# Second-layer and first-layer products in three float32r passes in place of a Strassen scheme in fp32

## The chip, the cores and the metric

The kernel runs on one core of a Trainium2 chip. The metric is the device time of one execution in microseconds; the kernel before takes 351.21 us (median of three runs, 351.08 to 351.37). A core has TensorE (PE; PEld is its weight load), VectorE (DVE), ScalarE (ACT), GpSimd (POOL) and SyncE (SP, which here only issues DMAs). SBUF is the working memory, 128 partitions wide; PSUM, in eight banks of 128 x 512 fp32, takes the results of TensorE.

## The reference

A Mamba-2 scan over 4 batches, 8 heads and 768 steps (head width 32, state width 16) makes a matrix of 3072 tokens by 256, and that goes through a feed-forward pair with SiLU between.

```python
for c in range(nc):
    cum = np.cumsum(log_a[:, :, sl], axis=-1)
    L = np.exp(cum[..., :, None] - cum[..., None, :]) * causal
    y_intra = einsum('bhij,bhjd->bhid', (Cc @ Bc^T) * L, xc)
    y_inter = einsum('bhin,bhnd->bhid', Cc, state) * exp(cum)[..., None]
    y[:, :, sl] = y_intra + y_inter
    state = decay_full * state + sum_j(Bc * xc * decay_from_j)
x = y.transpose(0, 2, 1, 3).reshape(3072, 256)
h = x @ w_in                       # 256 -> 2048
out = (h / (1 + np.exp(-h))) @ w_out   # 2048 -> 256
```

The two weights are given as 64-bit floats. The kernel loads their 32-bit words and rebuilds fp32 values on the chip.

## The kernel before

The tokens are cut into twelve **units** of 256 tokens (three a batch), and these into six **pairs**. Each unit passes three stages: the scan, which leaves `XM` (the 256 features by 256 tokens of the unit); the first layer with SiLU, which leaves `gT` (2048 by 256); and the second layer, whose result is transposed and stored.

The **scan** of a unit is a chain over all engines. `f_E0` clamps the decays `a` and `f_E1` makes the decay products E by scan instructions (L304); `f_P0`, `f_P1` make prefix products (L285, L291); `f_T` transposes B and C (L347) or, for units 0 to 2, `f_TP` does it on TensorE (L356); `f_B` and `f_C` scale them on GpSimd (L341, L373); `f_D0` and `f_G0` are the small products on TensorE (L391, L406); `f_S` carries the state (L432); `f_M` multiplies the mask in (L417); `f_Y` has the last products (L460, L469), and `f_X` copies the result out of PSUM (L482). One PSUM tile of four banks, `gy`, serves all of this.

The **weights** come in sixteen pieces, eight of `w_in` and eight of `w_out`. `load_w` issues one DMA of 512 KB for a piece (L156). `w_size` takes the exponent half and the mantissa half on ScalarE (L164, L168). `w_bits` has three VectorE steps (L176, L178, L180) and one GpSimd add (L184). At most seven raw pieces are in memory (`RAW = 7`): the load of piece n + 7 stands behind `w_bits(n)`, and waits for it.

The **first layer** of units 0 to 3 is plain (`f_s1`, L505): per group of 256 of the 2048 features four fp32 products, then one SiLU from PSUM (L507). From pair 2 on `f_x1` takes the two units of a pair as a 2 x 2 block matrix and uses Strassen's seven products in place of eight (L703), with sums of weights (`f_SW`) and sums of inputs (`f_XT`, L686) made beforehand; the results are put together by adds from PSUM (L706), ScalarE copies (L717) and SiLU (L709).

The **second layer** is Strassen's scheme for all six pairs (`s2_pair`, L611 and L648): seven chains of eight products. It needs sums of `gT`: `f_T1` makes TN on VectorE (L544), and `f_TS` adds blocks in place, mostly by a DMA of GpSimd's queue that accumulates (L553). The seven results are copied out (L588), added on GpSimd (L558), transposed by VectorE (L564) and stored from SP (L566). The last pair's chains are arranged to end in short pieces (L626 to L639).

The order is written out by hand (`manual_schedule`): each engine takes its instructions in the order in which the Python code reaches them. Up to L867 the scan of units 0 and 1, the first weight pieces and the first groups are interleaved. The list `steps` (L869) then gives for each first-layer group of units 0 and 1 what follows it: `s6` is `w_size(6)`, `b5` is `w_bits(5)`, letters are stages of unit 2's scan. After that, two loops of eight and one over the pairs 2 to 5 mix the first layer of a pair, the second layer of the pair before (`f_s2(n)` gives n of its products) and the scan of the next one. `load_unit(u)` puts a unit's eleven to seventeen loads on SP's queue. All of SP's DMAs run in order, and a DMA waits until the one eight places earlier has landed.

Of the kernel before, what the change touches and what calls it, by code (L numbers as in the profile page):

```python
# [8 lines left out]
FP32 = mybir.dt.float32  # L9
U32 = mybir.dt.uint32  # L10
# [7 lines left out]
MOST = 2.0 ** 16 * (1.875 - 2.0 ** -22)  # L18


@with_exitstack
def kernel(
# [10 lines left out]

# [4 lines left out]
    Q = 64  # L49
    UT = 256  # L50
    UPB = S // UT
    NU = batch * UPB
    d_model, d_ff = moe_w_in.shape
# [5 lines left out]
    loads = ctx.enter_context(tc.tile_pool(name="loads", bufs=3))  # L59
    loads2 = ctx.enter_context(tc.tile_pool(name="loads2", bufs=2))  # L60
    rawp = ctx.enter_context(tc.tile_pool(name="rawp", bufs=7))
    wtp = ctx.enter_context(tc.tile_pool(name="wtp", bufs=3))
    sc = ctx.enter_context(tc.tile_pool(name="sc", bufs=1))
    sc2 = ctx.enter_context(tc.tile_pool(name="sc2", bufs=2))
    xmp = ctx.enter_context(tc.tile_pool(name="xmp", bufs=4))
    gpool = ctx.enter_context(tc.tile_pool(name="gpool", bufs=4))
    tpool = ctx.enter_context(tc.tile_pool(name="tpool", bufs=1))
    ppool = ctx.enter_context(tc.tile_pool(name="ppool", bufs=5))
    opool = ctx.enter_context(tc.tile_pool(name="opool", bufs=2))
    ps_s = ctx.enter_context(tc.tile_pool(name="ps_s", bufs=1, space=bass.MemoryType.PSUM))  # L70
    ps_h = ctx.enter_context(tc.tile_pool(name="ps_h", bufs=3, space=bass.MemoryType.PSUM))
    ps_o = ctx.enter_context(tc.tile_pool(name="ps_o", bufs=1, space=bass.MemoryType.PSUM))

    ctx.enter_context(tc.manual_schedule())


    pa, ab, bn, tbc, xt = ({} for _ in range(5))
# [4 lines left out]
    def load_pa(u, q):  # L82

        b, t0 = at(u)
        pa[u] = loads.tile([128, UT], FP32, name="pa")
# [3 lines left out]
    def load_ab(u, q):  # L89

        b, t0 = at(u)
        ab[u] = loads2.tile([128, 2, H, Q], FP32, name="ab")
# [6 lines left out]
    def load_n(u, i, q):  # L99

        b, t0 = at(u)
        if i == 0:
            t = bn[u] = loads.tile([128, 2, H, N], FP32, name="bn")
        else:
            t = tbc[u] = loads.tile([128, 2, 2, 8, N], FP32, name="tbc")[:, 0]
# [3 lines left out]
    def load_t(u, i, q):  # L109

        b, t0 = at(u)
        if u not in tbc:
            tbc[u] = loads.tile([128, 2, 2, 8, N], FP32, name="tbc")
# [4 lines left out]
    def load_x(u, q):  # L118
        b, t0 = at(u)
        xt[u] = loads.tile([128, 2, H, D], FP32, name="xt")  # L120
# [3 lines left out]
    def load_unit(u):  # L124
        load_pa(u, nc.sync)
        if 0 < u < UPB:
            load_n(u, 1, nc.sync)
        else:
            load_t(u, 0, nc.sync)
            load_t(u, 1, nc.sync)  # L130
# [39 lines left out]
    def w_bits(n, parts=1):  # L170
# [14 lines left out]
        if n + RAW < len(W):  # L185
            load_w(n + RAW, nc.sync)

# [820 lines left out]
```

## Time and profile before

| what | value |
|---|---|
| median of three runs | 351.21 us (351.08 to 351.37) |
| span of the profiled execution | 348.7 us |
| TensorE busy | 342.7 us, 98% |
| VectorE, ScalarE, GpSimd busy | 204.6, 162.8, 113.0 us |
| DMA traffic | 42.66 MB, 16.25 MB of it on GpSimd's queue |

The span runs from the first to the last instruction; the time measured for a run is 2.5 us above it, and the profiled execution's own time beside that is not recorded. In the profile a line such as `69.80 1.73 PE hp L505 x8` gives start, length, engine, tile written, line and count. An fp32 product appears as two records, so x8 is four products. A group's mean duration is that of single instructions, which overlap on TensorE: there the distance from start to start is the price. What stands in brackets is the idle time before, and what ended it.

### The profile page before, as it was taken

How to read it: one execution, taken by the hardware profiler on the slowest of the kernel's cores; microseconds unless marked ns; L12 is line 12 of the kernel's file. 1: busy time of each engine (PE TensorE's matmuls, PEld its weight loads, DVE VectorE, ACT ScalarE, POOL GpSimd, SP SyncE). 2: the span in 40 equal slices, each digit the busy share in tenths (PEclk: the TensorE clock that was granted, in tenths of full speed). 3: DMA queues.
4: the chain of work that ended last, by engine and by line, in shares of the span. 5: the costliest groups of instructions: out<-in, count | busy, mean ns of one | idle time of the engine just before them, and what ended most of it. 6: DMA issues, size and time to landing. Idle time of an engine off the chain costs nothing.

```text
span 348.7 us, 8382 instructions
## 1 busy us (share of the span) xinstructions
PE 342.7 (98%) x3324; PEld 288.5 (83%) x3324; DVE 204.6 (59%) x406; ACT 162.8 (47%) x399; POOL 113.0 (32%) x140
## 2 busy tenths in 40 slices
PE   8999999999999999999999999999999999999996
PEld 3678888888888888888888888888888888888886
DVE  7998799976795664544663563564652241233912
ACT  3578395323323545455645454644545454454010
POOL 4355245444285032244042244042235112041200
DMA  6877997799857598948178965056604237512202
GB/s 130 203 237 174 241 313 126 132 199 218 144 102 126 124 186 149 169 102 138 21 159 163 187 112 90 16 98 125 115 2 75 39 60 144 107 24 53 41 7 46
DMA packets 117056, 42.66 MB, mean 122 GB/s; under 512 B 102424, under 2 KB 108824, under 8 KB 117016
## 3 DMA queue, kind: packets, MB, share of 16 engines
q1 hardware_dynamic: 110472, 25.73, 35.8%
q0 software_dynamic: 4464, 16.25, 25.0%
q8 instruction: 26, 0.43, 0.6%
q10 hardware_dynamic: 2080, 0.13, 0.4%
q14 instruction: 14, 0.11, 0.1%
HBM read 22.70 MB, written 3.15 MB: 74 GB/s over the span
## 4 chain that ended last, share of the span: by engine, by line
PE 96%; DVE 1%; issue 1%; POOL 1%; ACT 0%; DVEq 0%; POOLq 0%
PE o_ps L648 36%; PE hp L703 28%; PE hp L505 16%; PE hp L648 3%; PE gy L469 2%; PE gy L406 2%; PE o_ps L611 2%; PE gy L460 2%; PE gy L391 1%; PE hp L626 1%; PE hp L312 1%; PE o_ps L226 1%; POOL w_in_sb L184 1%; DVE E L417 0%; PE o_ps L228 0%
## 5 line engine op out<-in xcount | busy, mean ns | idle before, releaser
L706 DVE TENSOR_TENSOR gT<-hp,p 128x256 f32<-128x256 f32 x64 | 26.9, 420 | 73.6 <-ACT p L717 37.6
L648 PE MATMUL o_ps<-gT,w_out_sb 128*128 128x256 f32 x240 | 60.4, 379 | 0.0
L709 ACT ACTIVATE gT<-gT 128x256 f32<-128x256 f32 x96 | 39.7, 414 | 43.9 <-DVE gT L706 43.9
L505 PE MATMUL hp<-XM,w_in_sb 128*128 128x256 f32 x256 | 59.3, 381 | 0.9 <-ACT XM L482 0.5
L505 PEld LDWEIGHTS hp<-XM,w_in_sb 128*128 128x128 f32 x256 | 48.0, 190 | 8.7 <-POOL w_in_sb L184 1.4
L703 PE MATMUL hp<-raw 128*128 128x256 f32 x192 | 52.7, 380 | 0.0
L558 POOL TENSOR_TENSOR ps<-ps 128x256 f32<-128x256 f32 x35 | 29.6, 845 | 71.1 <-ACT ps L588 69.8
L648 PEld LDWEIGHTS o_ps<-gT,w_out_sb 128*128 128x128 f32 x240 | 45.4, 190 | 6.3
L553 POOL DMA_DIRECT2D gT<-gT x31 | 27.9, 929 | 65.7 <-DVE TN L544 21.5
L703 PEld LDWEIGHTS hp<-raw 128*128 128x128 f32 x192 | 36.2, 190 | 5.4 <-POOL ps L558 0.6
L717 ACT ACTIVATE p<-hp 128x256 f32<-128x256 f32 x64 | 24.6, 384 | 27.4 <-PE hp L703 25.9
L706 DVE TENSOR_TENSOR gT<-hp,u 128x256 f32<-128x256 f32 x32 | 13.6, 424 | 38.6 <-PE hp L703 38.6
L703 PE MATMUL hp<-XM,w_in_sb 128*128 128x256 f32 x128 | 34.1, 389 | 0.0
L507 ACT ACTIVATE gT<-hp 128x512 f32<-128x512 f32 x32 | 18.9, 595 | 26.4 <-PE hp L505 26.3
L703 PEld LDWEIGHTS hp<-XM,w_in_sb 128*128 128x128 f32 x128 | 23.3, 190 | 4.3 <-issue 1.0
L304 DVE TENSOR_TENSOR_SCAN E<-ab,diag 128x256 f32<-128x256 f32 (+1 forms) x32 | 25.1, 826 | 0.8 <-DVE ab L323 0.5
L341 POOL TENSOR_TENSOR BT<-bn,E 128x256 f32<-128x256 f32 x12 | 9.4, 780 | 47.5 <-DVE E L304 39.4
L648 PE MATMUL o_ps<-gT,wu 128*128 128x256 f32 x88 | 22.4, 380 | 0.0
L648 PE MATMUL o_ps<-gT,wv 128*128 128x256 f32 x88 | 22.2, 380 | 0.0
L648 PE MATMUL o_ps<-gT,raw 128*128 128x256 f32 x80 | 20.5, 380 | 0.0
L588 ACT ACTIVATE ps<-o_ps 128x256 f32<-128x256 f32 x35 | 13.3, 383 | 14.8 <-PE o_ps L648 13.0
L703 PE MATMUL hp<-raw,w_in_sb 128*128 128x256 f32 x64 | 19.1, 380 | 0.0
(126 smaller groups left out, 522.3 us busy)
## 6 DMA issues: line engine op xcount, KB each, us to landing
gT<-gT POOLq DMA_DIRECT2D x31, 512.0 KB, 6.3
ab<-in_a_dram SPq DMA_DIRECT2D x40, 128.0 KB, 3.1
raw<-in_moe_w_in_dram SPq DMA_DIRECT2D x8, 512.0 KB, 5.1
raw<-in_moe_w_out_dram SPq DMA_DIRECT2D x8, 512.0 KB, 6.5
xt<-in_x_dram SPq DMA_DIRECT2D x24, 128.0 KB, 5.1
out_dram<-ot SPq DMA_DIRECT2D x92, 32.0 KB, 2.6
bn<-in_B_dram SPq DMA_DIRECT2D x22, 64.0 KB, 5.3
tbc<-in_C_dram SPq DMA_DIRECT2D x40, 32.0 KB, 3.4
```

The source lines that it names most:

```text
L304: nc.vector.tensor_tensor_scan(out=E[u].rearrange("p k h t -> p (k h t)")[:, Q * g0:Q * (g0 + n)], data0=t.rearrange("p g t -> p (g t)"), ...
L341: engine.tensor_tensor(out=BT[u], in0=bn[u], in1=E[u][:, :, :, Q - 1:Q].to_broadcast([128, 2, H, N]), op=ALU.mult)
L505: nc.tensor.matmul(out=hp[:, i], lhsT=w_in_sb[:, kc, f * 128:(f + 1) * 128], rhs=xm[:, kc], start=(kc == 0), stop=(kc == KC - 1))
L507: nc.scalar.activation(GTS[g][:, :, j], hp, AF.Silu)
L553: nc.gpsimd.dma_start(out=o[:, js], in_=a[:, js], accum_op=ALU.add)
L558: engine.tensor_tensor(out=o, in0=p, in1=q, op=op)
L588: nc.scalar.activation(p[m].rearrange("p (k c t) -> p c k t", c=2, k=2), o.rearrange("p (c k t) -> p c k t", c=2, k=2), AF.Copy)
L648: nc.tensor.matmul(out=o, lhsT=w(j), rhs=g()[:, j], start=(j == 0), stop=(j == last))
L703: nc.tensor.matmul(out=o, lhsT=w, rhs=x_, start=start, stop=True, skip_group_check=True)
L706: nc.vector.tensor_tensor(out=o, in0=p, in1=q, op=ALU.add)
L709: nc.scalar.activation(o, i, AF.Silu)
L717: nc.scalar.activation(o, i, AF.Copy)
```

## The change

The units, the scan's arithmetic and the rebuilding of the weights stay. Strassen's scheme goes in both layers. Pair 0 uses plain fp32 products in both layers (`f_s1` L463, `f_s2` L476). For the pairs 1 to 5 every operand is cut into parts of 12 bits that a float32r product can take exactly. For a weight w: `wh` is w times a scale, rounded to float32r (ScalarE, L178), `wl` is the rest (VectorE, L182), and `wd` is `wh - wl` (GpSimd, L186). For an activation: `XH`, `XL`, `XD` in the first layer (L444, L448, L452) and `GH`, `GL`, `GD` in the second (L538 or L540, L544, L546). The sum is then made of three products, `wd*XD`, `wh*XH` and `wl*XL`, of 512 columns each: the two units of a pair side by side. As the parts have different scales, the PSUM bank is rescaled in place by ScalarE between them: in the first layer once for each 128 features (L524), in the second layer after each half of the 16 chunks and between its parts (L557).

PSUM now has two banks for the first layer (three before) and two for the second (one before). SBUF tiles of 128 x 512 come from one pool of 77. The clamp of the decays moves from VectorE to GpSimd (L301), and E is made in place of its input. Raw weight pieces come as two DMAs of 256 KB, at most six pieces are asked for in advance (`RAW = 6`), and piece n + 6 is issued where `w_bits(n)` stands. Stores take 128 x 512 tiles (L494, L496).

The order is new too. `steps` has the digits of `w_in` (`D0` to `D7`) and unit 3's scan in the stage of pair 0; half of pair 0's second layer follows, the other half lies beside the first four of pair 1's sixteen groups, as do `D8` to `D15` beside its first eight. From there each group has the first product `ff1_r` of the next group, the other two of its own (`ff1_p`), the digits of the group before (`g_h`, `g_ld`), one of eight steps of a later unit's scan, and five to seven products of the second layer (`quota`), which runs five groups behind.

```diff
-    rawp = ctx.enter_context(tc.tile_pool(name="rawp", bufs=7))
-    ps_h = ctx.enter_context(tc.tile_pool(name="ps_h", bufs=3, space=bass.MemoryType.PSUM))
-    ps_o = ctx.enter_context(tc.tile_pool(name="ps_o", bufs=1, space=bass.MemoryType.PSUM))
+    ps_h = ctx.enter_context(tc.tile_pool(name="ps_h", bufs=2, space=bass.MemoryType.PSUM))
+    ps_o = ctx.enter_context(tc.tile_pool(name="ps_o", bufs=2, space=bass.MemoryType.PSUM))
...
-    RAW = 7
+    RAW = 6
...
+        raw[n] = [t2("raw").bitcast(U32).rearrange("p (f two) -> p f two", two=2) for k in range(2)]
+        for k in range(2):
+            q.dma_start(out=raw[n][k].rearrange("p f two -> p (f two)"), in_=src[:, k].bitcast(U32))
...
+    def w_h(n):
+        nc.scalar.activation(wh[n], w32[n], AF.Copy, scale=HS / BB)
+    def w_l(n):
+        nc.vector.scalar_tensor_tensor(out=wl[n], in0=f32(wh[n]), scalar=-BB, in1=w32[n], op0=ALU.mult, op1=ALU.add)
+    def w_d(n):
+        nc.gpsimd.tensor_tensor(out=wd[n], in0=f32(wh[n]), in1=f32(wl[n]), op=ALU.subtract)
...
-        nc.vector.tensor_scalar(out=t, in0=t, scalar1=1.0, scalar2=1e-6, op0=ALU.min, op1=ALU.max)
-        nc.vector.memset(t[:, :, 0:1], 0.0)
+        nc.gpsimd.tensor_scalar(out=t, in0=t, scalar1=1.0, scalar2=1e-6, op0=ALU.min, op1=ALU.max)
+        nc.gpsimd.memset(t[:, :, 0:1], 0.0)
...
+    def f_XH(u):
+        nc.scalar.activation(XH[p][:, :, v], XM[u], AF.Copy, scale=HS)
+    def f_XL(u):
+        nc.gpsimd.tensor_tensor(out=XL[p][:, :, v], in0=XM[u], in1=f32(XH[p][:, :, v]), op=ALU.subtract)
+    def f_XD(u):
+        nc.vector.scalar_tensor_tensor(out=XD[p][:, :, v], in0=f32(XH[p][:, :, v]), scalar=-CC, in1=XM.pop(u),
+                                       op0=ALU.mult, op1=ALU.add)
...
+    def ff1_r(p, j):
+        o = HP[p, j] = ps_h.tile([128, 512], FP32, name="hp")
+        for kc in range(KC):
+            nc.tensor.matmul(out=o, lhsT=w1(wd, j, kc), rhs=xx(XD, p, kc), start=(kc == 0), stop=(kc == KC - 1),
+                             skip_group_check=True)
+        nc.scalar.activation(o, o, AF.Copy, scale=1.0 / CC)
+    def ff1_p(p, j):
+        o = HP.pop((p, j))
+        for n, (w, v) in enumerate(((wh, XH), (wl, XL))):
+            for kc in range(KC):
+                nc.tensor.matmul(out=o, lhsT=w1(w, j, kc), rhs=xx(v, p, kc), start=False, stop=(n + kc == 2),
+                                 skip_group_check=True)
+        A[p, j] = t2("ga")
+        nc.scalar.activation(A[p, j], o, AF.Silu, scale=BB * CC)
+    def g_h(p, j):
+        GH[p, j] = t2("gh", F32R)
+        if j % 2:
+            nc.vector.tensor_scalar(out=GH[p, j], in0=A[p, j], scalar1=HS, scalar2=None, op0=ALU.mult)
+        else:
+            nc.scalar.activation(GH[p, j], A[p, j], AF.Copy, scale=HS)
+    def g_ld(p, j):
+        nc.gpsimd.tensor_tensor(out=GL[p, j], in0=A[p, j], in1=f32(GH[p, j]), op=ALU.subtract)
+        nc.vector.scalar_tensor_tensor(out=GD[p, j], in0=f32(GH[p, j]), scalar=-CC, in1=A.pop((p, j)),
+                                       op0=ALU.mult, op1=ALU.add)
+    def ff2(p):
...
+            for c, m in order:
+                mm(wh, GH[p, c], c, m, start=(c == 0))
+                yield
+                mm(wl, GL[p, c], c, m)
+                if c == cs[-1]:
+                    scale(m, CC)
+                yield
+            for m in range(2):
+                for c in cs:
+                    mm(wd, GD[p, c], c, m)
+                    if c == cs[-1]:
+                        if half:
+                            f_out(p, m, o[m], BB)
+                        else:
+                            scale(m, 1.0 / CC)
+                    yield
...
-    steps = ((1, 0, ""), (0, 3, "b5 s6"), (1, 1, "b6 s7"), (1, 2, "b7 s8"), (1, 3, "b8"), (0, 4, ""),
-             (1, 4, "T"), (0, 5, "E D s9"), (1, 5, "C b9 s10"), (0, 6, ""), (1, 6, "G b10 s11"),
-             (0, 7, "b11 s12"), (1, 7, "Y b12 s13"))
+    steps = ((1, 0, ""), (0, 3, "b5 s6"), (1, 1, "b6 s7"), (1, 2, "L3 b7 s8"), (1, 3, "b8 s9 P2"), (0, 4, "T2 D0"),
+             (1, 4, "E2 D1"), (0, 5, "b9 s10"), (1, 5, "D2 G2"), (0, 6, "b10 s11 D3"), (1, 6, "P3 Y2"),
+             (0, 7, "T3 D4"), (1, 7, "E3 D5"))
...
+    for c, what in enumerate(("b11 s12", "D6 G3", "b12 s13", "D7", "Y3", "b13 s14", "b14 s15", "b15")):
+        f_s2(c)
+        todo(what)
```

## The prediction

> **What bounds the kernel now.** First the page: engine shares, the 40 slices, the chain's shares. Then groups split by shape, for the duration of every operation named below. Then the chain in order of time, for the length of one pair of units. Then the time order of VectorE, GpSimd, ScalarE and the DMA queue from 20 to 70 us, because the slices show VectorE near full there.
>
> ```profile
> PE 342.7 (98%) x3324; PEld 288.5 (83%) x3324; DVE 204.6 (59%) x406; ACT 162.8 (47%) x399; POOL 113.0 (32%) x140
> PE   8999999999999999999999999999999999999996
> DVE  7998799976795664544663563564652241233912
> PE 96%; DVE 1%; issue 1%; POOL 1%; ACT 0%; DVEq 0%; POOLq 0%
> ```
>
> TensorE is the bound from end to end; VectorE is nearly full only in the first fifth.
>
> ```profile
> 69.80 1.73 PE hp L505 x8
> 131.56 1.06 PE hp L703 x4
> 185.57 1.06 PE hp L703 x4
> 239.50 1.06 PE hp L703 x4
> ```
>
> Eight records in 1.73 us are 0.2157 us each. An fp32 product with 256 columns has two records: 0.431 us. Equal points of three pairs lie 54.01 and 53.93 us apart. A Strassen pair's 112 products are 48.3 us and its two units' scans 2 x 2.42 (1.00 for L391 and L406, 1.42 for L460 and L469, by their starts); some 0.8 is left.
>
> ```profile
> 47.68 0.42 DVE L176 TENSOR_SCALAR wu<-wu 128x512 f32<-128x512 f32 x1
> 48.13 0.43 DVE L178 TENSOR_SCALAR wu<-wu 128x512 uint32<-128x512 uint32 x1
> 49.08 0.42 DVE L176 TENSOR_SCALAR wu<-wu 128x512 f32<-128x512 f32 x1
> 49.53 1.39 DVE L178 TENSOR_SCALAR wu<-wu 128x512 uint32<-128x512 uint32 x1
> ```
> ```profile
> 49.24 1.40 POOL L184 TENSOR_TENSOR w_out_sb<-wu,wv 128x512 uint32<-128x512 uint32 x1 [2.32 <-DVE wv L180]
> ```
>
> The same VectorE instruction takes 0.43 us alone and 1.39 when a GpSimd add (1.40) begins before it: it waits for the rest of that add, some 0.95.
>
> ```profile
> 24.15 0.42 SPq L156 DMA_DIRECT2D raw<-in_moe_w_out_dram  x1
> 24.62 1.35 SPq L86 DMA_DIRECT2D pa<-in_a_dram  x1
> 28.80 4.91 SPq L107 DMA_DIRECT2D bn<-in_B_dram  x2
> 37.90 4.99 SPq L156 DMA_DIRECT2D raw<-in_moe_w_out_dram  x7
> ```
> ```profile
> 43.37 0.67 ACT L164 ACTIVATE wu<-raw 128x512 f32<-128x512 f32 x1 [3.35 <-DMA raw<-in_moe_w_out_dram]
> ```
>
> Weight piece 8 goes out at 24.15, then unit 2's loads take 13 us of SP's queue, and piece 9 goes out at 37.90 and lands 5.5 us later, with ScalarE waiting 3.35.
>
> **Products.** Before there are 688 fp32 products (four units' first layer of 64 per pair, 56 per Strassen pair of each layer): 296.7 us. After, pair 0 has 128 plain ones (55.2 us) and each of the five other pairs 16 x 6 + 16 x 2 x 3 = 192 float32r products of 512 columns. No row shows float32r. Its floor is the one-pass bf16 128x512 (three in 0.81 us, L226, 0.22 each); its ceiling the fp32 record, two array steps a column, 0.43 for 512. I take one pass, 0.2157: with operands of 12 bits one pass is all that the sum needs, and each fp32 record already carries two of four. Then 207.1 us, together 262.3: **-34.5** (pair 0 +3.5, pair 1 -10.4, the others -6.9 each). The ceiling is a rival below. Weight loads (190 ns, L648) stay under a 0.216 us product as now; were they not hidden, 960 x at most 0.19.
>
> The Trainium skill, "FP8 and Floating Point Precision", on precision, says that true FP32 takes four passes and that a reduced form reads 4-byte values cut to 22 bits; four passes agree with 0.431 us. By its reduced form a 512-column product would cost a quarter of the pass time, 0.216 us.
>
> **The first pair.** It ends where the first float32r product (L522) starts. For TensorE alone: from 15.04 us, 16 first-layer groups of 1.73 (27.7), eight second-layer chunks of 1.73 (13.8), scans of units 1 to 3 (7.3), transposes and the present gaps some 1.8: 65.6 us. VectorE will be later, for two reasons.
>
> (a) Piece 8. Raw pieces in flight fall from 7 to 6, so in program order piece 8 now stands behind unit 2's eleven loads. They took 24.62 to 37.90 in the queue; without piece 8's 0.5 MB, up to 2.4 us less at the 218 GB/s of 10 to 20 us. So it is issued at 35.1 to 37.5 and lands 5.5 later, 41.8. ScalarE's piece-8 step stands ahead of the SiLU of group (1,3), at about 33.8, so ScalarE waits some 8 us, and with two PSUM banks for the first layer in place of three TensorE stops one group later. VectorE, done with piece 7 at 34 to 35, waits too. Piece 8's first VectorE step then starts at 42.3.
>
> (b) VectorE's list from there to the masked product of unit 3 (L379): four pieces at 1.5 unblocked (6.0), two prefix scans (2.0), seven low-part steps L182 priced by L180 (0.60 each by starts: 4.2), eight scans of E (4.9), C 0.35, two transposes 1.1, states 1.8, four masked products 2.4, one XD 0.6: 23.4. GpSimd now also makes wd, XL and the clamp of E (L301), so eleven of these steps find it at work: nine at 0.95 and two at 0.5, 9.6. Waiting for ScalarE's first wh, 1.8. Sum 34.8, so 77.1. Behind it stand unit 3's Y (1.4) and three chunks (5.2): L522 starts at 83.7, **+18** over 65.6. The floor is +5 (piece 8 on time and steps with two SBUF inputs not blocked), the ceiling +22 (all of it, the clamp at the 2.35 of the 1024-wide GpSimd add; its floor is twice the 0.67 affine_select, 1.3).
>
> **Pair 1.** Groups 4 to 7 (no fp32 chunks beside them: 1.3, 2.6, 3.6, 2.8 us of TensorE) still carry wl and wd. GpSimd: four GL and four wd at 1.28, BT and CW 1.3, clamp 1.3, and 3 us of waiting: 15.8 against 10.3. Up to one group (2.6) is covered by the distance from GL to its use: **+3**, between 0 and +5.
>
> **Pairs 2 to 5.** Per group 12 products, 2.59 us. Per pair, TensorE 46.3. ScalarE: 16 x (rescale 0.60, SiLU 0.60, half the high parts 0.30) by L507, six PSUM passes 3.6, scan copies 6.3: 34. No row writes PSUM from ScalarE; below 0.60 no row goes, and 0.1 more each would be 1.6 a pair, hidden: ten products (2.16 us) lie between L522 and L530 of the same group. VectorE: GD 16 x 0.68, GH 8 x 0.42, scans and the rest 17.5: 32. GpSimd: 16 GL and two XL at 1.28, four small 2.6, two clamps 2.6: 28. Each alone is hidden. Blocked time: 38 VectorE steps, GpSimd at work half the time, half an add left on average, 11 us; VectorE then 43 of 46.3. That is nearly full, and Y waits for VectorE's masked product, so I take 0.5 us a pair: **+2**, between 0 and 29 (if all 24 us of GpSimd's reads block VectorE: 53.5 a pair, +7.2 on four).
>
> The Trainium skill, "SBUF — State Buffer", section on the shared port pair, says that a VectorE step with two SBUF inputs and a GpSimd step that reads SBUF exclude each other for a whole instruction. It speaks against this change, which feeds both engines the same two tiles (GL and GD). The rows show it for tensor_scalar (0.43 to 1.39) and adds (L544, 0.68 to 1.23), not for L180's form; with the rule for all forms the sum stands as given, without it (b) loses some 3 us.
>
> **The end.** Before, the last product is followed by one 0.29 add and a store. After: a 0.60 ScalarE copy, a 512-wide transpose (twice 0.43), four stores of 64 KB queued behind each other, where two took 1.21 to issue: **+2.5**, between +1 and +3.5.
>
> **Removed and hidden.** 31 accumulating DMAs of GpSimd's queue, 24 TN adds, 96 adds from PSUM, 64 + 32 copies: all lay beside TensorE, worth 0. Stores are 48 of 64 KB for 94 of up to 32; weights 32 of 256 KB for 16 of 512.
>
> **Sum.** Span 348.7 - 34.5 + 18 + 3 + 2 + 2.5 = 339.7. The runs' median, 351.2, is 2.5 above this execution's span; the same is added: **342**.
>
> **Rivals.**
> 1. Hardly a stall: +5, 0, 0, +1: span 320, time 323. For it: all tiles of the start have fresh memory, so loads queue only behind loads. Against it: VectorE has 9.8 of 10 us busy from 50 to 70 even now.
> 2. Slower: the port shared by VectorE and GpSimd becomes the bound of pairs 2 to 5, with 29 in place of 2: 369. It decides from +11 us on these pairs, 2.7 a pair. For it: GpSimd goes from 113 us to about 190, VectorE to some 220 without waits. Against it: unblocked sums leave 14 us a pair.
> 3. float32r runs at the fp32 record's two steps a column: +207 us hides all stalls: 348.7 - 34.5 + 207 + 2.5 = 524. Against it: the two steps are two passes, not reading.
>
> **Chances.** Forecast case (328 to 350) 0.62; rival 1 0.14; no change (within 0.2%, what a measurement of this kernel can tell) 0.02; rival 2 and lesser forms of it 0.17; rival 3 0.05. Faster 0.76, same 0.02, slower 0.22. The range 324 to 360 leaves out rival 3 (0.05), the upper half of rival 2 (0.08) and the lower half of rival 1 (0.07).
>
> **What will show it.** L522, L530 and L554 at 0.216 us by starts. The first L522 at 80 to 86 us, ScalarE idle 6 to 9 us before an L153 on a raw load, near 34 to 42. L182 and L546 at two values, 0.68 and over 1. TensorE without gaps over 0.5 us in pairs 2 to 5, pairs 47 us apart. Wrong if L522 starts before 75, if gaps ahead of L420 in pairs 2 to 5 sum to over 5, or if a float32r product takes 0.43.

## The result and the profile after

The changed kernel takes 372.9 us (median of four runs, 372.1 to 373.9), against 351.1 for the kernel before on the same chip. The ratio is 1.063, 95% interval 1.060 to 1.066: 6.3% slower. The prediction was 342 (324 to 360) and faster. The profiled span is 372.2 us, 32.5 above the predicted 339.7; it belongs to the longest of the four runs (373.9), so span and time lie 1.7 us apart here, where the prediction took 2.5.

The page after: engine shares, three rows of the 40 slices (9.3 us each), and the shares of the chain that ended last.

```profile
PE 331.8 (89%) x3145; PEld 261.3 (70%) x3146; DVE 271.5 (73%) x391; ACT 208.1 (56%) x425; POOL 224.2 (60%) x180
...
PE   8789589399995797899989989989999899999993
...
DVE  7897498968759966795893975985976956575431
...
PEclk9999699699998888999999999999999999999997
...
PE 49%; issue 13%; POOL 12%; DVE 11%; SPq 5%; DMA 4%; ACT 4%; POOLq 0%; DVEq 0%; ACTq 0%
```

TensorE was 98% busy and 96% of the chain; now it is 89% and 49%. It stands still for over 2 us in five places of the first 150 us, each with a low clock at its end or behind it (PEclk), and a little in each unit after. A stop is given below as the idle time that the profile has in brackets.

The price of a float32r product: TensorE in time order, start, length, engine, line.

```profile
238.77 0.39 PE L554 MATMUL o_ps<-gl,wl 128*128 128x512 f32 x1
238.99 0.39 PE L554 MATMUL o_ps<-gh,wh 128*128 128x512 f32 x1
239.22 0.39 PE L554 MATMUL o_ps<-gl,wl 128*128 128x512 f32 x1
239.45 0.39 PE L554 MATMUL o_ps<-gh,wh 128*128 128x512 f32 x1
```

Three steps from start to start in 0.68 us: 0.2267 each, where the prediction had 0.2157. That is about half of the 0.431 of a whole fp32 product, for twice its columns: one pass, a little slower than a pass of before.

The first pair: the DMA queue, ScalarE and TensorE in time order.

```profile
36.12 5.26 SPq L146 DMA_DIRECT2D raw<-in_moe_w_out_dram  x10
...
39.70 0.43 ACT L153 ACTIVATE wu<-raw 128x256 f32<-128x256 f32 x1 [4.72 <-DMA raw<-in_moe_w_out_dram]
...
41.95 8.12 PE L463 MATMUL hp<-XM,w 128*128 128x256 f32 x24 [3.89 <-ACT g L466]
...
70.77 0.68 PE L355 MATMUL gy<-xt,BT 64*32 64x64 f32 x32 [5.93 <-POOL BT L310]
...
85.33 1.28 PE L522 MATMUL hp<-xd,wd 128*128 128x512 f32 x4
```

Piece 8 goes out at 36.1 and ScalarE waits 4.7 us for it; TensorE stops for 3.9, and its next 24 records take 0.34 us each, not 0.216. A second stop of 5.9 stands before D0 of unit 3 (L355). The first float32r product starts at 85.3. In the twelve profiled kernels that leave the first pair as it is, this one included, that start lies between 83.7 and 86.2.

Pair 1, TensorE:

```profile
117.88 0.46 PE L355 MATMUL gy<-xt,BT 64*32 64x64 f32 x32 [3.96 <-POOL BT L310]
...
118.89 1.07 PE L522 MATMUL hp<-xd,wd 128*128 128x512 f32 x2
...
129.41 1.13 PE L411 MATMUL gy<-cw,sm 32*64 32x64 f32 x32 [2.71 <-DVE ab L379]
...
143.16 0.65 PE L355 MATMUL gy<-xt,BT 64*32 64x64 f32 x24 [2.36 <-POOL BT L310]
```

In the pairs 2 to 5 one unit in steady state (ACT, DVE, POOL, PE, each engine in time order by itself):

```profile
236.02 0.60 ACT L533 ACTIVATE ga<-hp 128x512 f32<-128x512 f32 x1 [0.32 <-PE hp L530]
...
234.63 1.82 DVE L546 SCALAR_TENSOR_TENSOR gd<-gh,ga 128x512 fp32r<-128x512 f32 x1
236.37 1.38 DVE L267 TENSOR_SCALAR pz<-pa 128x256 f32<-128x256 f32 x1
...
240.17 0.40 DVE L538 TENSOR_SCALAR gh<-ga 128x512 fp32r<-128x512 f32 x1
240.67 1.81 DVE L546 SCALAR_TENSOR_TENSOR gd<-gh,ga 128x512 fp32r<-128x512 f32 x1
...
242.41 1.26 DVE L282 TENSOR_TENSOR_SCAN ab<-ab,diag 128x256 f32<-128x256 f32 x2
...
240.65 1.29 POOL L544 TENSOR_TENSOR gl<-ga,gh 128x512 fp32r<-128x512 f32 x1 [3.05 <-DVE gh L538]
243.75 1.00 POOL L310 TENSOR_TENSOR BT<-bn,ab 128x256 f32<-128x256 f32 x1 [1.81 <-DVE ab L282]
...
244.81 0.46 PE L355 MATMUL gy<-xt,BT 64*32 64x64 f32 x32 [1.37 <-POOL BT L310]
```

Read it from the bottom: D0 waits for BT, BT for the last scans of E (L282), these stand behind GD, GD behind GH, and GH behind VectorE's own earlier steps. The SiLU (L533) that this GH reads had ended at 236.6, so GH came 3.6 us late; VectorE is not idle for over 0.2 us at a time from 230.6 to 245. GD is stretched from 0.67 to 1.81 beside GL on GpSimd. In the units 6 to 11 GH of groups 7 and 15 comes 2.4 to 3.6 us after its SiLU, and one stop of 0.4 to 1.4 us at D0 follows in each.

The 32.5 us by place (here alone a stop counts from start to start, less one product): products 960 x 0.011 = 10.6; the first float32r product 1.6; pair 1, from the first L522 to Y of unit 6, some 14 more than the 3 predicted (six stops, 12.4, and about 4.4 in which the products after the three long ones run at up to 0.43); units 7 to 11 at 26.15 us against 24.77 in the kernels below that have no stop there, 6.9, so 5 more than predicted; the end 0.8. Together 32; what is left is not placed.

### The profile page after: what moved, and what is told of

Read it like the earlier page. It is cut to its first block, busy times and chain, and to the rows that moved or that the text cites. A ratio compares the mean times of both kernels' runs of the same rounds, so it can differ in the third digit from the quotient of the medians.

```text
span 372.2 us, 8081 instructions
## 1 busy us (share of the span) xinstructions
PE 331.8 (89%) x3145; PEld 261.3 (70%) x3146; DVE 271.5 (73%) x391; ACT 208.1 (56%) x425; POOL 224.2 (60%) x180
## 4 chain that ended last, share of the span: by engine, by line
PE 49%; issue 13%; POOL 12%; DVE 11%; SPq 5%; DMA 4%; ACT 4%; POOLq 0%; DVEq 0%; ACTq 0%
PE o_ps L554 13%; PE hp L530 11%; POOL gl L544 7%; PE o_ps L476 7%; PE hp L522 6%; DVE ab L282 3%; POOL BT L310 2%; PE gy L420 2%; PE gy L369 2%; DVE wl L182 2%; PE gy L411 2%; PE hp L463 2%; PE hp L289 1%; SPq L92 1%; DVE gd L546 1%
## 5 line engine op out<-in xcount | busy, mean ns | idle before, releaser
L544 POOL TENSOR_TENSOR gl<-ga,gh 128x512 fp32r<-128x512 f32 x80 | 125.4, 1574 | 47.3 <-DVE gh L538 22.6
L546 DVE SCALAR_TENSOR_TENSOR gd<-gh,ga 128x512 fp32r<-128x512 f32 x80 | 87.2, 1090 | 29.0 <-ACT gh L540 24.1
L524 ACT ACTIVATE hp<-hp 128x512 f32<-128x512 f32 x80 | 46.5, 582 | 82.5 <-PE hp L522 82.5
L554 PE MATMUL o_ps<-gl,wl 128*128 128x512 f32 x160 | 63.0, 394 | 0.0
L554 PE MATMUL o_ps<-gh,wh 128*128 128x512 f32 x160 | 62.7, 392 | 0.0
L533 ACT ACTIVATE ga<-hp 128x512 f32<-128x512 f32 x80 | 47.8, 597 | 23.5 <-PE hp L530 22.4
L522 PE MATMUL hp<-xd,wd 128*128 128x512 f32 x160 | 54.3, 422 | 2.1 <-DVE xd L452 1.3
L530 PE MATMUL hp<-xh,wh 128*128 128x512 f32 x160 | 50.5, 397 | 0.2 <-ACT hp L524 0.2
L530 PE MATMUL hp<-xl,wl 128*128 128x512 f32 x160 | 49.9, 393 | 0.0
L554 PE MATMUL o_ps<-gd,wd 128*128 128x512 f32 x160 | 41.1, 391 | 0.1
L463 PE MATMUL hp<-XM,w 128*128 128x256 f32 x128 | 32.0, 409 | 5.9 <-ACT g L466 3.9
L522 PEld LDWEIGHTS hp<-xd,wd 128*128 128x128 f32 x160 | 28.6, 191 | 11.7 <-ACT ga L533 3.4
L538 DVE TENSOR_SCALAR gh<-ga 128x512 fp32r<-128x512 f32 x40 | 26.9, 673 | 9.6 <-ACT ga L533 9.4
L463 PEld LDWEIGHTS hp<-XM,w 128*128 128x128 f32 x128 | 25.7, 205 | 11.3 <-ACT g L466 4.1
L448 POOL TENSOR_TENSOR xl<-XM,xh 128x512 fp32r<-128x512 f32 x10 | 17.7, 1772 | 23.9 <-ACT xh L444 23.9
L186 POOL TENSOR_TENSOR wd<-wh,wl 128x512 fp32r<-128x512 f32 x16 | 23.6, 1472 | 12.7 <-DVE wl L182 11.4
```

The lines of the kernel that those rows point to most:

```text
L186: nc.gpsimd.tensor_tensor(out=wd[n], in0=f32(wh[n]), in1=f32(wl[n]), op=ALU.subtract)
L463: nc.tensor.matmul(out=hp[:, i], lhsT=w32[j][:, kc, 128 * i:128 * i + 128], rhs=XM[u][:, kc], start=(kc == 0), stop=(kc == KC - 1))
L522: nc.tensor.matmul(out=o, lhsT=w1(wd, j, kc), rhs=xx(XD, p, kc), start=(kc == 0), stop=(kc == KC - 1), skip_group_check=True)
L524: nc.scalar.activation(o, o, AF.Copy, scale=1.0 / CC)
L530: nc.tensor.matmul(out=o, lhsT=w1(w, j, kc), rhs=xx(v, p, kc), start=False, stop=(n + kc == 2), skip_group_check=True)
L533: nc.scalar.activation(A[p, j], o, AF.Silu, scale=BB * CC)
```

## The experiments

In all of them "theory" and "rival" are as the expectation names them. Times are to be set against 372.9 for the changed kernel; the kernel before ran at 350.4 to 351.5 beside them.

**The price of a product.** Each first product of a group in two halves:

```diff
-            nc.tensor.matmul(out=o, lhsT=w1(wd, j, kc), rhs=xx(XD, p, kc), ...)
+            for h in (slice(0, 256), slice(256, 512)):
+                nc.tensor.matmul(out=o[:, h], lhsT=w1(wd, j, kc), rhs=xx(XD, p, kc)[:, h], ...)
```

> The first product of each group (L522) in two halves of 256 columns with the same weights, so that the load of the weights stands beside half as many columns. If a float32r product of 512 columns (0.2267 by starts) is columns and a fixed part, a half takes 0.11 to 0.13; if the load of 128 x 128 weights in four bytes is what it waits for, 0.19 to 0.21 a half. Under the first the kernel gets at most 3 us longer, under the second 10 to 14.

373.4 us in one run. TensorE and its weight loads in time order (lines one further down):

```profile
201.62 0.64 PE L523 MATMUL hp<-xd,wd 128*128 128x256 f32 x4
202.09 0.63 PE L531 MATMUL hp<-xh,wh 128*128 128x512 f32 x2
...
201.40 0.65 PEld L523 LDWEIGHTS hp<-xd,wd 128*128 128x128 f32 x4
```

Four halves in 0.47 us, 0.118 each. With 0.2267 for 512 that is 0.425 ns a column and some 0.009 us for each product (a line through two points, which no third one tests). Each half has a weight load of its own, 0.19 long, and four of these take 0.65: they overlap, and a product of 512 columns does not wait for them.

**The first pair.** Unit 2's loads behind piece 8:

```diff
-    load_unit(2)
     f_s1(0, 0)
...
     w_bits(2, 2)
+    load_unit(2)
```

> One edit to the changed kernel: unit 2's loads are issued after those of weight piece 8, not before them. Theory 1 (ScalarE's wait for piece 8 makes the stop of 3.9 us and the slow clock after it, and everything behind it moves with it, as VectorE is full from 42 to 77 us): the ACT wait of 4.7 us at L153 goes, the first L522 starts at 79 to 82 in place of 85.3, the time falls by 3 to 6. Rival (VectorE's list of 50 to 77 us, or unit 2's later data, sets the end of the first pair): the first L522 stays after 84 and the time within 1.5 us of 373.

372.3 us (371.1 to 373.5). The first L522 stands at 82.4 in the profiled execution, 1.3 us ahead of the earliest of the twelve above, but the median is only 0.7 us lower, within the scatter. Stops of 1.7, 2.4 and 5.4 us stay; later pieces now wait behind unit 2's loads. Piece 8 alone was not what held the first pair.

Unit 3's scan ahead of the weight part D4:

```diff
-             (0, 7, "T3 D4"), (1, 7, "E3 D5"))
+             (0, 7, "T3"), (1, 7, "E3 D4 D5"))
...
-    ("b11 s12", "D6 G3", "b12 s13", "D7", "Y3", "b13 s14", ...)
+    ("b11 s12", "D6 G3", "X2 b12 s13", "D7", "Y3 X3", "b13 s14", ...)
```

`X` holds XH, XL and XD, which stood in `Y` before.

> One edit to the changed kernel, in the first pair alone: unit 3's transposes and scans of E go ahead of the weight parts D4, and XH, XL and XD of unit 2 go behind them. Theory 2 (order, not amount): BT of unit 3 is done at 66.5 to 68 in place of 70.7, the stop of TensorE ahead of D0 (6.3 us) shrinks to 2 to 4, and the first L522 stands at 80.5 to 83 in place of 84 to 85.3; the time falls by 2 to 5. Rival (the amount of VectorE's work up to Y of unit 3 sets the end of the first pair, as the prediction had it): the stop moves to Y or to the first L522, which stays at 84 to 86, and the time stays within 1.5 us of 373.

368.6 us (367.9 to 369.5), 4.3 less. GpSimd and TensorE:

```profile
64.47 0.94 POOL L310 TENSOR_TENSOR BT<-bn,ab 128x256 f32<-128x256 f32 x1 [2.61 <-DVE ab L282]
...
65.46 0.46 PE L355 MATMUL gy<-xt,BT 64*32 64x64 f32 x32 [0.86 <-POOL BT L310]
```

BT of unit 3 is done 5 us earlier, the stop falls from 5.9 to 0.9 us, and the first L522 stands at 79.4 (85.3). No work was taken away: here the order was the cause. The prediction's sum of VectorE's list counted all of it as standing before Y of unit 3, as it does in the changed kernel; some of it did not need to.

**Pairs 2 to 5, first round.** The scan's step ahead of GL and GD:

```diff
-        if s > 16:
-            g_ld(*before)
-        stores()
         tasks = plan.get(s, [])
         for pre, post in tasks:
             for f in pre:
                 f()
+        if s > 16:
+            g_ld(*before)
+        stores()
```

> One edit to the changed kernel: from pair 1 on the scan's step of a group is issued ahead of GL and GD of that group, so that the scans of E (L282), BT and CW no longer stand behind them on VectorE and GpSimd. Theory 1 (TensorE's in-order waits at D0 come from the chain E, BT behind the mutually blocked GD and GL): the gap ahead of D0 (L355; 0.75 to 1.76 us, 3.1 a pair in pairs 2 to 5, and 3.96 and 2.36 in pair 1) falls under 0.4, and the time falls by 8 to 14 us, to 359 to 365. Rival (the amount of VectorE's work is the bound, whatever its order): the gaps only move, and the time stays within 2 us of 373.

406.0 us (404.1 to 407.5): theory and rival both fell. GpSimd and TensorE:

```profile
228.70 1.94 POOL L310 TENSOR_TENSOR BT<-bn,ab 128x256 f32<-128x256 f32 x1 [3.91 <-DVE ab L282]
...
232.54 0.74 PE L554 MATMUL o_ps<-gl,wl 128*128 128x512 f32 x1 [4.55 <-POOL gl L544]
```

GL now stands on GpSimd behind a BT that waits for E, and the second layer reads that GL in the next group. One in-order queue carries two chains that both end within one group, and whichever stands behind is late.

GL on VectorE, so that GpSimd reads nothing beside GD:

```diff
-        nc.gpsimd.tensor_tensor(out=GL[p, j], in0=A[p, j], in1=f32(GH[p, j]), op=ALU.subtract)
+        nc.vector.tensor_tensor(out=GL[p, j], in0=A[p, j], in1=f32(GH[p, j]), op=ALU.subtract)
```

> One edit to the changed kernel: GL (L544) moves from GpSimd to VectorE, 80 instructions; GpSimd no longer reads the tiles that VectorE reads for GD. Theory 1 (the exclusion of VectorE and GpSimd is what costs): GD at 0.68 nearly everywhere (mean 1.09 now), scans of E under 1 us, gaps ahead of D0 under 0.4; VectorE gets 16 x 0.68 = 10.9 us a pair and loses about 8 of blocked time, so that its busy time of 40.7 in a pair hardly rises; the time falls by 6 to 12, to 361 to 367. Rival (VectorE's own amount of work): it is busy over 48 us in a pair, the gaps grow and the time rises, to 375 to 385.

374.8 us (372.3 to 375.3). The groups of VectorE from 165 to 360 us, changed kernel and then this one (count, busy, mean ns, idle before):

```profile
L546 DVE SCALAR_TENSOR_TENSOR gd<-gh,ga 128x512 fp32r<-128x512 f32 x64 | 67.4, 1053 | 25.0 <-ACT gh L540 20.9 <-issue 1.4
```
```profile
L546 DVE SCALAR_TENSOR_TENSOR gd<-gh,ga 128x512 fp32r<-128x512 f32 x64 | 50.7, 792 | 0.0
L544 DVE TENSOR_TENSOR gl<-ga,gh 128x512 fp32r<-128x512 f32 x64 | 48.1, 752 | 20.6 <-ACT gh L540 18.3
```

GD loses a quarter of its time, and with GL on it VectorE is busy for only some 3 us a pair more. The time lies just under the rival's 375 to 385, with VectorE busy for 43 us a pair and not 48; the gain that the theory forecast did not come. By place, the units run at 25.96 us (26.15), 0.9 less over five, and pair 1 takes 88.3 (87.1). The run takes the blocking away and gives VectorE the work at once, so it prices neither alone.

E one step earlier in the scan:

```diff
-  1: P0, P1, T2     2: E1(0), E1(1), T2              3: E1(2), E1(3), B, C
+  1: E1(0), E1(1), T2   2: E1(2), E1(3), P0, P1, T2   3: B, C
```

> One edit to the changed kernel: in the pairs 1 to 5 the four scans of E stand one step of the unit's scan earlier (steps 1 and 2 in place of 2 and 3), the prefix product goes to step 2, and step 3 holds only BT and CW; GD and GL stay ahead of a group's step. Theory 2 (the wait at D0 is a distance too short: SiLU, GH, GD, two scans and BT follow one another within one group, so the order ahead of BT counts and not the sum of VectorE's work, nor the exclusion): BT follows GL on GpSimd without the wait for E of 1.8 us, the gaps ahead of L355 in pairs 2 to 5 fall from 1.3 to 1.8 to under 0.4, and the time falls by 7 to 13 us, to 360 to 366. Rival (VectorE's amount): the gaps move to the last products of Y (L411) or to L554, and the time stays within 2 us of 373.

371.2 us (369.7 to 371.8). That is 1.8 less. The stops at D0 are gone in the pairs 2 to 5, and another has come (VectorE, GpSimd, TensorE):

```profile
239.28 0.40 DVE L538 TENSOR_SCALAR gh<-ga 128x512 fp32r<-128x512 f32 x1
...
239.77 1.27 POOL L544 TENSOR_TENSOR gl<-ga,gh 128x512 fp32r<-128x512 f32 x1 [4.22 <-DVE gh L538]
...
241.09 0.50 PE L554 MATMUL o_ps<-gl,wl 128*128 128x512 f32 x1 [0.84 <-POOL gl L544]
```

It is GL of group 7, made in the group before the one that reads it. The wait for BT had hidden this second chain: 25.89 us a unit.

The quota changed on top of that, so that chunks 7 and 15 are read later in their group:

```diff
-(6, 6, 7, 7, 6, 5, 5, 6, 6, 6, 7, 7, 6, 5, 5, 6)
+(4, 6, 6, 5, 7, 7, 7, 6, 4, 6, 6, 5, 7, 7, 7, 6)
```

> The kernel with E one step earlier, and one more edit: the second layer's products of a half are given out as 4, 6, 6, 5, 7, 7, 7, 6 over eight groups in place of 6, 6, 7, 7, 6, 5, 5, 6, so that chunk 7 and chunk 15, whose GL is made in the group just before, are read some five products (1.1 us) later. Theory 3 (each way from SiLU to the product, and from E to D0, had less than one group's distance, and what came first hid the other): the new waits of L554 for GL (1.35 and 0.87 us a unit) go too, pairs 2 to 5 run at 50.0 to 50.8 a pair, and the time falls by another 6 to 9 from 371.2, to 362 to 365. Rival (VectorE or GpSimd cannot do more): the wait moves to another place and the time stays within 2 us of 371.

376.4 us (375.4 to 378.1), 5 more, and 27.0 us a unit; one of the five units, at 28.8, holds a stretch at half clock (0.50 from 243.5 to 246.9 us), the others run at 26.1 to 27.2. The group in which BT is made has five products in place of seven, so TensorE comes to D0 earlier (stops of 0.54), and GL is still late (up to 1.2). The cure was wrong: products are the distance, and these were taken from the group that needed them.

The same with GL on VectorE (the diff of L544 above added):

> The kernel with E one step earlier and the new quota, and GL on VectorE in place of GpSimd. It asks whether the exclusion of the two engines has a price of its own once the distances are long enough. If the exclusion is only dangerous where a chain is short: within 2 us of the same kernel with GL on GpSimd (362 to 365). If blocked time itself costs: 3 to 6 us faster. If VectorE's amount is near the bound: 3 or more slower.

377.1 us (376.1 to 378.8), within 1 us of the time with GL on GpSimd. But the places differ: the units run at 26.3 us (27.0), 3.6 less over five, some of it the stretch at half clock, and pair 1, where VectorE has the weight parts too, takes 89.4 (85.3). So this does not show that the exclusion costs nothing; what the units gained was lost in pair 1.

**Pairs 2 to 5, the link.** GH always by ScalarE:

```diff
-        if j % 2:
+        if False:
             nc.vector.tensor_scalar(out=GH[p, j], in0=A[p, j], scalar1=HS, scalar2=None, op0=ALU.mult)
         else:
             nc.scalar.activation(GH[p, j], A[p, j], AF.Copy, scale=HS)
```

> One edit to the changed kernel: GH is always made by ScalarE; the eight groups of a pair whose GH VectorE made (L538) lose that step, chunks 7 and 15 among them. Theory 4 (in pairs 2 to 5 the waits come from VectorE's and GpSimd's order around chunks 7 and 15: GH on VectorE comes late behind the scan's steps, GL behind GH, E behind GD): BT no longer waits 1.8 us for E, the gaps at D0 fall from 1.3 to 1.8 to 0.2 to 0.9, pairs 2 to 5 run at 50.5 to 51.5 (52.3 now), time 366 to 370. Rival (E stands one group too late, and only moving it helps): gaps at D0 stay over 1.0 and the time within 2 us of 373.

362.4 us (362.2 to 363.9): 10.5 less by one line. The same 104.4 us of the span (four units of the changed kernel, a little more of this one), changed kernel and then this one (PE, PEld, DVE, ACT, POOL busy, clock, DMA share, GB/s):

```profile
190.80:295.20 104.40, 99.80 (x1009) 78.85 (x1008) 80.27 (x112) 64.42 (x125) 69.19 (x52) 1.00 0.27 49
```
```profile
190.80:295.20 104.40, 103.45 (x1097) 82.31 (x1090) 73.49 (x95) 75.45 (x146) 70.91 (x53) 1.00 0.26 47
```

TensorE is busy for 3.7 us more of the 104.4, VectorE for 6.8 less and ScalarE for 11 more. GD's mean is still 1.00 us (1.05), so it is blocked nearly as before. What has changed is that GH follows SiLU on ScalarE, 0.3 us after it where it was 2.4 to 3.6, and no longer stands behind VectorE's scan steps with GD and E behind it. Units run at 25.09 us; pair 1 takes 81.1 (87.1).

GH of groups 7 and 15 alone:

```diff
-        if j % 2:
+        if j % 2 and j % 8 != 7:
```

> GH on ScalarE for the groups 7 and 15 only (two of the eight of a pair that VectorE made); all else as in the changed kernel. If the late GH of just these two groups, whose group also holds the last scans of E, made the waits (with all eight moved the time was 362.4): at least two thirds of the 10.5 us, 362 to 366, gaps at D0 0.4 to 0.9. If it was VectorE's amount of work (eight steps of 0.4 to 1.0 us a pair): about a quarter, 369 to 371.5, gaps still 1.0 to 1.6.

367.5 us (365.5 to 369.4), 25.65 a unit: 5.4 of the 10.5 us, between theory and rival. Two steps of eight bring half. The position of these two is worth about twice their share; the other half comes with the other six, and whether by their position too or by VectorE's load is not settled. Stops of 0.3 to 1.3 us at D0 stay.

E one step earlier and GH on ScalarE (two of the diffs above), old quota:

> E one step earlier and GH always on ScalarE, with the old quota. Theory 4: with both ways shortened no gap over 0.5 us is left in pairs 2 to 5, which run at 50.2 to 50.8 a pair, and the time is 361 to 365. Rival (the quota of the six-edit kernel did it): waits of L554 for GL of 0.8 us or more a unit stay, and the time is 368 to 372.

360.7 us (359.7 to 364.7). No stop over 0.5 us is left in the pairs 2 to 5: 24.76 us a unit, 49.5 a pair against 54.0 for a Strassen pair. TensorE is busy for all of the 104.4 us of that stretch.

**Pair 1.** D8 to D15 spread over the groups 1 to 14:

```diff
-        if p == 1 and digits and j < 8:
+        if p == 1 and j in (1, 3, 4, 6, 8, 10, 12, 14):
```

> One edit to the changed kernel: the parts D8 to D15 of the second layer's weights are made beside groups 1, 3, 4, 6, 8, 10, 12, 14 of pair 1 in place of 0 to 7. Theory 1 (wl and wd, packed into eight groups, fill VectorE and GpSimd from 107 to 120 us and delay unit 4's scan): the gaps of 4.3, 3.1 and 2.7 us at 113 to 142 shrink to under 2 each, and with them the slow clock; the time falls by 5 to 10. Rival (pair 1 waits for the same chain as the later pairs, GL and GD ahead of E and BT): the time falls by 0 to 3.

372.9 us (371.2 to 374.4). The stop at Y of unit 4 goes (2.7), that at D0 is 3.7 (4.0), one of 1.0 at Y of unit 5 comes and that at D0 of unit 6 grows from 0.4 to 1.4, and no time is won: pair 1 takes 85.8 (87.1) in the profiled execution, the median is the same. Theory fell.

The parts ahead of the plain chunks:

```diff
+        if p == 1 and digits and j < 8:
+            todo(digits.pop(0))
         if p == 1 and rest:
             ...
-        if p == 1 and digits and j < 8:
-            todo(digits.pop(0))
```

> One edit to the changed kernel, in pair 1 alone: the parts of a weight piece (D8 to D15) are issued ahead of the two plain chunks of the same group, not behind them, so that wh on ScalarE no longer stands behind the copies of pair 0's output (L489), which wait for the last plain chunk. Theory (order on ScalarE): VectorE's idle 3.7 us ahead of wl near 100 us goes, the stop at 113.5 (4.3) shrinks to 1 to 2.5, the time falls by 2 to 4. Rival (pair 1's groups without plain chunks are too short for their scan, whatever ScalarE's order): the stop stays above 3.5 us and the time within 1.5 of 373.

370.7 us (367.8 to 371.2), 2.3 less. The copy of pair 0's output on ScalarE in the changed kernel, and wh in its place in this one:

```profile
105.15 0.60 ACT L489 ACTIVATE pt<-o_ps 128x512 f32<-128x512 f32 x1 [1.60 <-PE o_ps L476]
```
```profile
103.47 0.62 ACT L178 ACTIVATE wh<-w 128x512 fp32r<-128x512 f32 x1
```

D0 of unit 4 stops for 1.1 (4.0), but Y of unit 4 now for 3.9 (2.7). ScalarE's order was one cause, and some 1.2 of the 2.9 us that it gave were lost at the next wait.

**All edits of order.** Piece 8, unit 3's scan, E earlier and D8 to D15 spread as above, and D0 and Y of unit 3 a chunk later:

```diff
-("b11 s12", "D6 G3", "X2 b12 s13", "D7", "Y3 X3", "b13 s14", ...)
+("b11 s12", "D6", "G3 X2 b12 s13", "D7", "", "Y3 X3 b13 s14", ...)
```

> Five edits to the changed kernel together: unit 2's loads behind piece 8, unit 3's scan ahead of D4, D0 of unit 3 and Y of unit 3 one chunk later, E one step earlier in the pairs 1 to 5, and D8 to D15 spread over groups 1 to 14. Theory 2 (order and distances): the gaps add up, 3 us from piece 8, 3 to 6 from unit 3, 3 to 5 from pair 1, 9 to 11 from the D0 gaps: 349 to 356, so about the time before the change. Rival (VectorE's amount): under 6 us are won, 367 to 373.

366.7 us (364.4 to 367.9), 6.2 less: the theory's sum fell; it took for cured what the earlier E and the spread parts do not cure. To these the new quota, GH on ScalarE, and these:

```diff
-(1, 3, "b8 s9 P2"), ... (1, 4, "E2 D1"), ... (1, 5, "D2 G2")
+(1, 3, "b8 P2"), ... (1, 4, "s9 E2 D1"), ... (1, 5, "G2 D2")
...
-((-3, 5) if p > 2 else (2, 7))
+((-3, 5) if p > 2 else (3, 6))
...
+        if p == 1 and j in (1, 3, 4, 6, 8, 10, 12, 14):
+            todo(digits.pop(0))
         if p == 1 and rest:
-            for c in rest[:2]:
+            n = 2 if j < 3 else 1
+            for c in rest[:n]:
```

> All edits of order together: those of the five-edit kernel, the new quota, the exponent half of piece 9 one group later, G of unit 2 ahead of D2, the last four plain chunks and the parts D8 to D15 so placed in pair 1 that the parts stand ahead of the chunks, unit 4's scan one group later and unit 5's one earlier, and GH always on ScalarE. Theory 3: pairs 2 to 5 at 50 to 50.8 (-8 against the five-edit kernel), first L522 at 73 to 76 (-2 to -4), pair 1's stops halved (-5 to -8): 347 to 353, about the time before the change. Rival (amount): over 360.

359.3 us (358.3 to 360.4), 25.2 a unit, between theory and rival. In pair 1 a new stop of 5.8 us (VectorE, TensorE):

```profile
111.05 3.41 DVE L282 TENSOR_TENSOR_SCAN ab<-ab,diag 128x256 f32<-128x256 f32 x2
...
117.74 1.26 DVE L282 TENSOR_TENSOR_SCAN ab<-ab,diag 128x256 f32<-128x256 f32 x2
...
121.02 0.68 DVE L379 TENSOR_TENSOR ab<-gy,ab 128x512 f32<-128x512 f32 x1
...
121.85 1.13 PE L411 MATMUL gy<-cw,sm 32*64 32x64 f32 x32 [5.77 <-DVE ab L379]
```

The second masked product of unit 4 stands behind unit 5's scans of E. Two kernels take that up, one with more changes in the first pair and in the place of pair 1's weight parts and the last stores on two queues, one with nothing else:

```diff
-  5: f_S, f_SM, f_M(0)      6: f_M(1), then f_Y
+  5: f_S, f_SM, f_M(0), f_M(1)      6: f_Y
...
-((-3, 5) if p > 2 else (3, 6))
+((-3, 5) if p > 2 else (3, 7))
```

> The kernel with all edits of order (359.3), changed further: both masked products in one step, unit 5's scan back at its place, unit 2's E ahead of pieces 8 and 9 and of the weight parts, D7 in pair 1, D8 to D11 in its first four groups beside the plain chunks, the last stores on two queues. Theory (order in the first pair and in pair 1, no amount): the stop at Y of unit 4 (6.3) falls under 3, the stop at D0 of unit 2 (3.4) goes, 1 us less at the end: 349 to 354. Rival (VectorE's and GpSimd's amount up to 160 us is what bounds the first two pairs): the stops move, and the time is 357 to 361.

> The kernel with all edits of order (359.3) and two more, in the scan's steps: both masked products in one step, ahead of the next unit's scans of E, and unit 5's scan back at its place. Theory (the second masked product of unit 4 stood behind unit 5's E): the stop at Y of unit 4 falls from 6.3 to 1.5 to 3, the time to 355 to 358. Rival (amount): the stop moves to another place and the time stays at 358 to 361.

356.4 us (353.6 to 358.8), between its theory and its rival, and 351.6 (349.8 to 353.2) for the smaller edit, less than the 355 to 358 that its theory gave: ratio to the kernel before 1.000, interval 0.998 to 1.003. The larger one stops for 3.7 us at D0 of unit 3 and for 2.7 at D0 of unit 5; which of its edits does that was not tried. Last, the smaller one with the old quota and a few edits more:

```diff
-(0, 4, "T2 D0"), (1, 4, "s9 E2 D1")
+(0, 4, "T2"), (1, 4, "E2 s9 D0 D1")
...
-        if after[0] < NP:
+        if after[0] < NP and s != 31:
             ff1_r(*after)
...
         f_ff2(quota.get(s, 0))
+        if s == 31:
+            ff1_r(*after)
...
-            nc.sync.dma_start(
+            (nc.scalar if p == NP - 1 and q % 2 else nc.sync).dma_start(
```

`D7` goes to group 2 of pair 1.

> The kernel at 351.6 with the old quota again and five more edits of order: E of unit 2 ahead of the weight parts D0, D7 in pair 1, the plain chunks of pair 1 unchanged but its parts beside groups 1 to 14 again, the first product of pair 2 behind the second-layer products of its group, the last stores on two queues. Terms: quota 8 units at 0.43 (25.20 to 24.77 a unit) -3.4; the waits ahead of D0 of unit 2 (2.3) and of the first product of pair 2 (2.7) -1 to -4; the end -1. Theory (order and distance): 342 to 347, 1 to 2.5% below the kernel before the change. Rival (at 351.6 the amount of work already binds): 349 to 352.

347.3 us (346.6 to 347.9); ratio to the kernel before 0.990, interval 0.987 to 0.992: one per cent below the kernel before, just above the theory's 342 to 347 and below the rival's 349 to 352. Its page:

```profile
PE 323.8 (94%) x3145; PEld 256.1 (74%) x3146; DVE 255.8 (74%) x351; ACT 229.6 (66%) x465; POOL 228.6 (66%) x180
...
PE   8889969889998989799999999999999999999992
DVE  6998899998499998977967949948959844333411
...
PE 66%; DVE 10%; SPq 10%; DMA 4%; issue 4%; POOL 3%; ACT 1%; DVEq 0%; POOLq 0%; ACTq 0%
```

From 153 to 277 us TensorE does not stop at all. The first L522 is at 74.9, Y of unit 6 at 153.0 (172.5). VectorE is busy 24.6 of 25 us from 50 to 75, the time for which GpSimd blocks it included, so there its amount may bind now; no run tests that. About 9 us over the 65.6 of TensorE alone are left.

## Why the prediction was wrong

The sign was wrong; the range ended at 360 and missed by 13 us. Of the 32.5 us that the span is off, 14 are in pair 1, 10.6 in the price of a product and 5 in the pairs 2 to 5.

- **Products, -34.5: mis-sized.** One pass was right, the rival of 0.43 fell. The step taken over from fp32 records, 0.2157, is 0.2267: -23.9. That weight loads stay under a product held, as the halves show.
- **The first pair, +18: right in size.** Piece 8 was issued at 36.1 (35.1 to 37.5 predicted), its first half landed at 39.7 (41.8), the first L522 stood at 85.3 (83.7, and 83.7 to 86.2 is what the same first pair scatters by). But the step "(b)" took VectorE's list as one block up to the masked product and had TensorE wait behind that; the stop of 5.9 us stands at D0, for BT, and before Y (78.9) there is none. Unit 3's E put ahead of D4 alone won 4.3 us.
- **Pair 1, +3: the step that failed.** It added up GpSimd's time for groups 4 to 7 and took one group of cover from GL to its use. It never looked at the chain: GH behind VectorE's earlier steps, GD behind GH, E behind GD, BT behind E, D0 behind BT, the masked product behind other scans, wh behind the copy of pair 0's output. Measured some 17, of which 4.4 are products slowed after a stop, which the sum did not have at all.
- **Pairs 2 to 5, +2: failed in the same way.** Sums of 28 to 43 of 46 us a pair were taken to say that "each alone is hidden". VectorE's was near enough (80.3 in 104.4 us, 40.2 a pair with its blocked time, 43 predicted); GpSimd's was short, 34.7 a pair (69.2 in 104.4 us) for 28, as only VectorE was charged for blocking and GL took 1.57 on average, not 1.28. Both are under 46, and TensorE still stopped in every unit with a scan. Sums bound an engine; they don't say that a result is there in time.
- **The end, +2.5: right** (from the last product to the end 6.6 us, 3.3 more than before).
- **Removed and hidden, 0, and ScalarE's new steps:** nothing speaks against it; the rescale of a PSUM bank in place takes 0.58 us (0.60 taken). Two of the 94 stores of before are of 64 KB and not of up to 32, which changes nothing in the sum.
- **Rival 1 (323) fell** with the first two stops.
- **Rival 2 (369) came near the time by luck.** It put 29 us into the pairs 2 to 5 and decided from 11; these lost 7, and the rest came from places that it did not name. Its own terms, 32 and 24 us a pair on VectorE, make 56 and not the 53.5 that it went by, and would have given some 379. The long rows were as the prediction said: GD 0.67 and 1.81 beside GL. The Trainium skill, "SBUF — State Buffer", "Who interferes with whom", has two SBUF inputs on VectorE contend with a GpSimd step that reads SBUF, and this row agrees for that form. In the unit shown three blocked steps (1.82, 1.38 and 1.81 us, against 0.67, 0.28 and 0.67 alone) make VectorE's list 3.4 us longer ahead of the last E, more than the stop of 1.4 behind it, so contention has a part in that chain. But it did not become a bound: with GH on ScalarE GD is blocked as before and the stops at D0 fall to 0.4 or less. And taking it away with GL on VectorE left the time where it was, twice, since VectorE then did that work itself. What contention alone costs no run shows.
- Of the signs named for a wrong forecast, "gaps ahead of L420 in pairs 2 to 5 sum to over 5" did not come as written: none stands ahead of L420, but those at D0 of the units 7 to 11 sum to 6.0. The sign of a right one, pairs 47 us apart, failed: they are 52.3 apart, and 49.5 without any stop.

My first theory, that the exclusion alone made the stops, did not give its gain with GL on VectorE; the second, E a group too late, was only half of the link; the third, more distance by the quota, made it worse. GH on VectorE is shown by its own run. That the rest of the first half is held by order is shown for unit 3's scan, the copy of pair 0's output and, with unit 5's scan moved beside it, the masked product; for the remaining 9 us of the first pair VectorE's full rows speak for amount, which no run tested alone. That order cost most of the rest is shown by the sum: the last kernel has all products and steps of the changed one in another order, with GH on ScalarE and half of the last stores on a second queue, and is 25.6 us faster.

## What to carry to other kernels

When several in-order engines pass a result on, add up the chain from the last producer to its reader in the group where it is made, with what stands ahead of it in each queue, and compare it with the distance in time to the reader; busy shares of 56 to 73%, as VectorE, ScalarE and GpSimd have here, say nothing on that. Moving one late link shows the next one, so measure after each edit, and look first at the small step that sits between two long chains: here a multiplication of 0.4 us alone, eight times a pair on the wrong engine, cost 10 us in all. A faster product makes all those distances shorter, as the group that covers them is shorter.

## What the hardware showed that was not expected

- A float32r product of 512 columns takes 0.2267 us and one of 256 columns 0.118, by the halves 0.425 ns a column and about 0.009 us besides. The Trainium skill, "TensorE: Matmul & The Clock Gate", "Back-to-back issue gap", gives N / 2.4 + 2.5 ns for the gap of an isolated matmul at full clock; 215.8 ns for 512 columns is an estimate by that formula, which does not name the operand type. The float32r rows lie 5% above it, and the measurement decides.
- A long stop can cost more than itself. After 3.9 us (to 41.95) 24 fp32 records took 8.1 us in place of 5.2, with the granted clock at 0.66 from 40 to 50 us; after the 4.0 us stop in pair 1 eight float32r products ran at 0.43, with the clock at 0.50 from 119.1 to 122.5. The length of a stop alone does not say whether that comes: after the stop of 2.4 us at 143.2 the clock was 0.50 for 3.4 us, while in the kernel with GH on ScalarE a stop of 3.3 us at 41.1 passed with the clock at 1.00 from 36 to 66.
